# Wider mix pieces, sums over a whole row block, paired 64-row channel mixes, and output steps at later fixed places

## The chip, the cores and the metric

The kernel runs on one core of one Trainium2 chip. The metric is the device time of one execution in microseconds (us), as a median over the runs of a kernel. Engine names are those of the profile: PE is the matmul engine, PEld its weight loads, DVE the vector engine, ACT the scalar engine, POOL and SP the two engines that issue most DMAs.

## The reference

```python
# x: (8, 4224, 192) f32; weight: (8 heads, 7 taps); theta, ch: (192, 192); tok_r, tok_i: (4224, 4224)
w = softmax(weight, axis=-1)
x = causal 7-tap convolution of x along the sequence, one set of taps per head of 24 channels
theta = x @ w_theta
zr, zi = x * cos(theta), x * sin(theta)
y = einsum('ts,bsd->btd', w_tok_r, zr) + einsum('ts,bsd->btd', w_tok_i, zi)
u = x + y
out = u + maximum(u @ w_ch, 0)
```

The cost is in the two token mixes: for each of the 33 blocks of 128 output rows, matmuls over 4224 tokens (33 chunks of 128) against 1536 columns (8 batches times 192 channels), twice.

## The kernel before

The 33 chunks are done in three passes of 11, because `zr` and `zi` are kept for only 22 chunks at a time. Each pass goes over all 33 row blocks; partial sums go to memory between passes. The first row block of pass 1 builds its chunks as it goes; the chunks of pass 2 and pass 3 are built in the shade of the pass before. In the last pass the output work (add x, transpose, mix channels, relu, store) runs beside the token mix.

The parts that matter here, with cuts marked:

```python
PC = 2 * D                       # a piece is 384 columns (2 batches); NP = 4 pieces in a row block
PASSES = (11, 11, 11)

pe_last = [None]
def pe(ins):                     # all PE instructions keep the order in which they are written
    if pe_last[0] is not None:
        tc.add_manual_dep(ins.ins, pe_last[0].ins.name, NOSYNC, reason="order")
    pe_last[0] = ins
    return ins
# DVE has no such order: the scheduler of the framework chooses the order of its queue

def channel_weights(w, name):    # 192 rows of w as 4 slots of 128 rows; slots 1 and 2 padded with zeros
    R = D - P                    # 64
    t = constp.tile([P, 4, D], BF16, name=name)
    nc.vector.memset(t[:, 1:3, :], 0.0)
    # ... four DMAs: w[0:128], w[128:192] | w[0:64] in the lower half, w[64:192]
    return t

def channel_mix(dst, tT, w):     # 2 batches: 4 matmuls of 128 rows
    for b in range(2):
        for k in range(2):
            pe(nc.tensor.matmul(
                dst[:, b, :], lhsT=tT[:, b + k, :], rhs=w[:, 2 * b + k, :],
                start=(k == 0), stop=(k == 1),
            ))

def mix(y, wts, zs, c, j, ncs):  # one "mix step": chunk c of piece j, two matmuls
    # ...

def finish_piece(tb, j, y, p):
    # ... p == 0: copy y to ev, store; p == 1: load pv, ev = y + pv, store
    pv = wk.tile([P, PC], F32, name="pv", tag="pv", bufs=3)
    nc.sync.dma_start(out=pv, in_=part[p - 1][tb, :, cols])
    # ... last pass from here on:
    xr = wk.tile([P, PC], BF16, name="xr", tag="sn")
    nc.sync.dma_start(out=xr, in_=xs[rows, cols])
    nc.vector.tensor_tensor(out=pv, in0=pv, in1=xr, op=ALU.add)      # "the add"
    nc.vector.tensor_tensor(out=ev, in0=y, in1=pv, op=ALU.add)       # "the sum"
    ub = wk.tile([P, PC], BF16, name="ub", tag="cs")
    nc.scalar.activation(out=ub, in_=ev, func=AT.Copy)
    def transposes():            # 3 PE transposes of ub, DVE copies them to uT
        # ...
    def channels():              # channel_mix(v, uT, wch); ov = max(v, 0) + ev; store
        # ...
    return [transposes, channels]

# last pass: one output step half-way through a piece and one at its end
for c in range(ncs):
    mix(y, wts, zs[p], c, j, ncs)
    done += 1
    if pend and c in (ncs // 2, ncs - 1):
        pend.pop(0)()
    # ... cut
pend += finish_piece(tb, j, y, p)
```

Once per row block, DVE also transposes the mix weights of the next block (six instructions, `wt<-st`: four of 128x512 and two of 128x384).

## Time and profile before

| | us |
|---|---|
| median, the three runs given at first | 1712.29 |
| median, the same three and one more, set beside the changed kernel | 1710.88 (1706.91 to 1716.38) |
| profiled execution, span | 1714.9 |
| of it: first row block, with the first chunks' build | 119.2 |
| rest of pass 1 | 493.2 |
| pass 2 | 506.0 |
| last pass, to the start of the last PE instruction | 592.2 |
| tail, from that start to the end | 4.2 |

The stages are cut at the start of the mix matmul that begins each one. The page's first part gives the busy time of each engine with its share of the span and its instructions:

```profile
PE 1631.2 (95%) x11088; PEld 1004.9 (59%) x11088; DVE 886.7 (52%) x1737; ACT 237.2 (14%) x399; POOL 514.9 (30%) x948
```

The table of windows gives the same by stretch of time; its last three columns are the granted PE clock, the DMA share, and GB/s:

```profile
core 0: us, PE busy (x) PEld busy (x) DVE busy (x) ACT busy (x) POOL busy (x), PEclk, DMA share, GB/s
0.00:119.00 119.00, 76.68 (x572) 48.72 (x573) 75.50 (x146) 56.39 (x91) 55.52 (x104) 0.85 0.89 126
...
1118.00:1715.00 597.00, 555.67 (x3833) 342.94 (x3830) 344.29 (x720) 69.01 (x132) 130.72 (x244) 0.99 0.67 147
```

PE is full in the two middle stages (not shown) and idle for 42 us in the first and 41 us in the last. The list of waits names what PE and DVE waited for in the last pass (total us, times, longest):

```profile
PE tu L289 <- ACT ub L283: 24.8, 43, 2.2
PE v L225 <- DVE uT L290: 11.6, 32, 0.5
...
DVE pv L280 <- DMA pv<-part_84: 142.7, 96, 4.0
```

PE waits for the piece to be transposed and for the transposes to be copied. Behind both stands DVE, which waits for the load of `pv` in 96 of its 132 adds.

Busy time says little about PE, because matmuls overlap; the distance between starts says more. In the timeline (start, duration, engine, line, instruction, rows*columns of the weights, shape of what streams), a mix matmul of 384 columns starts 0.16 us after the one before. In the same trace are matmuls that use the array as two halves by columns (`96*64`), and each change of mode costs extra; a channel mix of two batches (`v`) has none:

```profile
420.70 0.33 PE L257 MATMUL y<-zi,wt_4149 128*128 128x384 bf16 x1
420.96 0.27 PE L170 MATMUL pc<-xw_3846,bands 96*64 96x192 bf16 x1
420.96 0.27 PE L170 MATMUL pc<-xw_3849,bands 96*64 96x192 bf16 x1
...
421.23 0.25 PE L170 MATMUL pc<-xw_3849,bands 96*64 96x192 bf16 x1
421.41 0.34 PE L257 MATMUL y<-zr,wt_4140 128*128 128x384 bf16 x1
...
1403.15 0.49 PE L225 MATMUL v<-wch,uT 128*128 128x192 bf16 x4
1403.48 0.33 PE L257 MATMUL y<-zr,wt_14563 128*128 128x384 bf16 x1
```

Over the whole trace the medians are: mix to mix 162.5 ns; a matmul of 192 columns to the next instruction 82.5 ns; a transpose 56 ns; mix to band matmul 256 ns where 162.5 would be normal; band to mix 178 ns where 82.5 would be. So each change of mode costs about 94 ns. The Trainium skill, "TensorE: Matmul & The Clock Gate", section Back-to-back issue gap, gives N/2.4 + 2.5 ns for N columns as the gap of isolated matmuls at the full clock; that is 162.5, 82.5 and 55.8 ns, which this trace agrees with.

These pitches add up to the time that the last pass would need without waits: 2904 mix matmuls of 162.5 ns, 396 transposes of 56 ns and 66 channel mixes at 660 ns (two mixes of two batches counted as one): 471.9 + 22.2 + 43.6 = 537.7 us. The pass takes 592.2 us, so about 54 us are waits.

### The profile page before, as it was taken

Reading aid. Unit: us, or ns where it says so; the run is one execution under the profiler, and the core shown is the slowest. Engines: PE = TensorE matmul, PEld = TensorE weight load, DVE = VectorE, ACT = ScalarE, POOL = GpSimd, SP = SyncE. Lnnn points to the kernel's source line nnn. Section 1 sums busy time; section 2 is a strip of 40 time slices with the busy share of each in tenths; the row PEclk is TensorE's granted clock in tenths of the full one; section 3 lists DMA queues with packets and bytes.
Section 4 is the critical chain, followed back from the end, with each engine's and each line's share of the span. In section 5 each row is a group of like instructions: output and inputs, shape, how many; then the busy total and the mean of one; then the engine's idle time right before and its main releaser. Section 6 shows DMA issues by size and latency. Waiting matters only on the chain. (4 is left out here: it accounts for less than half of the span.)

```text
span 1714.9 us, 28577 instructions
## 1 busy us (share of the span) xinstructions
PE 1631.2 (95%) x11088; PEld 1004.9 (59%) x11088; DVE 886.7 (52%) x1737; ACT 237.2 (14%) x399; POOL 514.9 (30%) x948
## 2 busy tenths in 40 slices
PE   4789999999999999999999999999999999999998
PEld 2446666666666666666666666655555555555555
DVE  6664444444444434444444444455565655656554
ACT  3541111111111001111111111001111111111111
POOL 6432333323333233333333223222122222221210
PEclk8889999999999999999999999999999999999999
DMA  9987766666666688878887877767677676676753
GB/s 120 138 135 139 125 118 124 120 123 117 116 114 121 119 161 175 164 173 172 181 177 165 172 161 161 163 149 153 151 150 154 149 152 152 144 158 149 155 134 97
DMA packets 305175, 248.75 MB, mean 145 GB/s; under 512 B 81168, under 2 KB 300816, under 8 KB 305040
## 3 DMA queue, kind: packets, MB, share of 16 engines
q0 software_dynamic: 167616, 91.14, 43.2%
q1 hardware_dynamic: 137424, 155.80, 28.8%
q8 instruction: 86, 1.41, 0.3%
q14 instruction: 49, 0.40, 0.1%
HBM read 247.07 MB, written 90.83 MB: 197 GB/s over the span
## 5 line engine op out<-in xcount | busy, mean ns | idle before, releaser
L238 POOL DMA_DIRECT2D st<-in_moe_w_tok_i_dram x396 | 212.8, 545 | 1006.2 <-DVE wt_15169 L247 14.5
L238 POOL DMA_DIRECT2D st<-in_moe_w_tok_r_dram x396 | 213.1, 546 | 10.8 <-issue 6.5
L215 ACT ACTIVATE cs<-ang,half_pi 128x768 bf16<-128x768 f32 x66 | 61.6, 933 | 653.6 <-DVE ang L208 653.5
L280 DVE TENSOR_TENSOR pv<-pv,xr 128x384 f32<-128x384 f32 x132 | 73.0, 553 | 147.3 <-DMA pv<-part_84 147.3
L283 ACT ACTIVATE ub<-ev 128x384 bf16<-128x384 f32 x132 | 69.0, 523 | 549.6 <-DVE ev L281 549.6
L275 DVE TENSOR_TENSOR ev<-y,pv 128x384 f32<-128x384 f32 x132 | 71.6, 542 | 137.4 <-PE y L257 133.0
L269 DVE COPY ev<-y 128x384 f32<-128x384 f32 x132 | 71.6, 542 | 135.5 <-PE y L257 135.3
L290 DVE COPY uT<-tu 128x384 bf16<-128x384 bf16 x132 | 46.0, 349 | 98.2 <-PE tu L289 98.2
L208 DVE TENSOR_SCALAR ang<-th 128x384 f32<-128x384 f32 x132 | 68.1, 549 | 51.7 <-PE th L225 49.9
L175 ACT ACTIVATE xz<-pc 128x384 bf16<-128x384 f32 x132 | 57.2, 485 | 262.7 <-PE pc L170 262.1
L225 PE MATMUL v<-wch,uT 128*128 128x192 bf16 x528 | 65.5, 247 | 11.6 <-DVE uT L290 11.6
L199 DVE COPY xT<-tp 128x768 bf16<-128x768 bf16 x66 | 36.4, 551 | 75.8 <-PE tp L195 75.5
L281 DVE TENSOR_TENSOR ev<-y,pv 128x384 f32<-128x384 f32 x132 | 72.2, 547 | 6.2 <-PE y L257 6.2
L296 DVE SCALAR_TENSOR_TENSOR ov<-v,ev 128x384 f32<-128x384 f32 x132 | 71.4, 541 | 0.6 <-PE v L225 0.6
L289 PE MATMUL tu<-ident,ub 128*128 128x128 bf16 x396 | 44.4, 221 | 25.7 <-ACT ub L283 24.8
L225 PEld LDWEIGHTS <-uT 128*128 128x128 bf16 x528 | 45.0, 98 | 36.7 <-DVE uT L290 23.7
L225 PE MATMUL th<-wth,xT 128*128 128x192 bf16 x528 | 61.5, 262 | 1.9 <-DVE ang L208 1.3
L289 PEld LDWEIGHTS <-ub 128*128 128x128 bf16 x396 | 28.0, 98 | 58.1 <-ACT ub L283 49.6
L225 PEld LDWEIGHTS <-xT 128*128 128x128 bf16 x528 | 50.4, 105 | 14.6 <-issue 7.0
L170 PEld LDWEIGHTS <-bands 96*64 96x64 bf16 x528 | 23.1, 112 | 54.6 <-issue 38.0
L216 ACT ACTIVATE sn<-ang 128x768 bf16<-128x768 f32 x66 | 54.6, 827 | 0.0
L217 DVE TENSOR_TENSOR zr<-xz,cs 128x768 bf16<-128x768 bf16 x66 | 36.6, 554 | 32.4 <-ACT cs L215 32.4
(761 smaller groups left out, 4336.7 us busy)
## 6 DMA issues: line engine op xcount, KB each, us to landing
st<-in_moe_w_tok_r_dram POOLq DMA_DIRECT2D x396, 88.0 KB, 5.0
st<-in_moe_w_tok_i_dram POOLq DMA_DIRECT2D x396, 88.0 KB, 3.5
part_83<-ev SPq DMA_DIRECT2D x132, 192.0 KB, 3.0
pv<-part_83 SPq DMA_DIRECT2D x132, 192.0 KB, 3.7
part_84<-ev SPq DMA_DIRECT2D x132, 192.0 KB, 3.3
pv<-part_84 SPq DMA_DIRECT2D x132, 192.0 KB, 2.6
out_dram<-ov SPq DMA_DIRECT2D x132, 192.0 KB, 2.6
xs<-xz SPq DMA_DIRECT2D x132, 96.0 KB, 4.1
```

The source lines that it names most:

```text
L175: nc.scalar.activation(out=xz[:, :, hp * 2 * G : (hp + 1) * 2 * G].rearrange("p b (h g) -> p h b g", h=2, g=G), in_=pc[:, :, :, :], func=A ...
L208: nc.vector.tensor_scalar(out=ang[:, k, :], in0=th[:, :, :].rearrange("p b d -> p (b d)"), scalar1=-CLAMP, scalar2=CLAMP, op0=ALU.max, op1 ...
L215: nc.scalar.activation(out=cs, in_=af, func=AT.Sin, bias=half_pi[:], scale=1.0)
L225: pe(nc.tensor.matmul(dst[:, b, :], lhsT=tT[:, b + k, :], rhs=w[:, 2 * b + k, :], start=(k == 0), stop=(k == 1),))
L238: nc.gpsimd.dma_start(out=st[a * Q : (a + 1) * Q, :, 0 : ncs * Q], in_=w[tb * P : (tb + 1) * P, t0 : t0 + ncs * Q].rearrange("(bt i) s -> ...
L269: nc.vector.tensor_copy(out=ev, in_=y)
L275: nc.vector.tensor_tensor(out=ev, in0=y, in1=pv, op=ALU.add)
L280: nc.vector.tensor_tensor(out=pv, in0=pv, in1=xr, op=ALU.add)
L281: nc.vector.tensor_tensor(out=ev, in0=y, in1=pv, op=ALU.add)
L283: nc.scalar.activation(out=ub, in_=ev, func=AT.Copy)
L289: pe(nc.tensor.transpose(tp[:, k, :], ub[:, k * P : (k + 1) * P], ident))
L296: nc.vector.scalar_tensor_tensor(out=ov, in0=v[:, :, :].rearrange("p b d -> p (b d)"), scalar=0.0, in1=ev, op0=ALU.max, op1=ALU.add,)
```

## The change

The intent has four parts. (1) A mix piece has 512 columns in place of 384: three pieces per row block and a quarter fewer matmuls. (2) `pv`, which holds the partial sums, is as wide as a row block, loaded ahead with one DMA, summed into in place and stored in two halves of four batches. The output steps of a row block stand at four fixed places, six to eight mix steps after their inputs. (3) A channel mix takes four batches. Where two batches' last 64 rows of contraction were padded to 128 with zeros, they are now two matmuls of 64 rows that can run side by side in the two halves of the array. (4) To fit, PSUM buffers go from 4+2+2 to 3+2x2+1 banks, so there is one buffer for transposes instead of two, and the clamp handles 768 columns at once.

The diff, cut to its core:

```diff
-    PC = 2 * D
+    PC = 512
 ...
-        t = constp.tile([P, 4, D], BF16, name=name)
-        nc.vector.memset(t[:, 1:3, :], 0.0)
+        t = constp.tile([P, 3, D], BF16, name=name)     # slot 1: 64 rows of each of the two cuts
 ...
-    trps = ctx.enter_context(tc.tile_pool(name="trps", bufs=2, space=bass.MemoryType.PSUM))
+    trps = ctx.enter_context(tc.tile_pool(name="trps", bufs=1, space=bass.MemoryType.PSUM))
 ...
     def channel_mix(dst, tT, w):
-        for b in range(2):
-            # 2 batches, 4 matmuls of 128 rows
+        R = D - P
+        for q in range(2):
+            v = [dst[:, k, q * D : (q + 1) * D] for k in range(2)]
+            for k in range(2):
+                pe(nc.tensor.matmul(
+                    v[k], lhsT=tT[:, 3 * q + 2 * k, :], rhs=w[:, 2 * k, :],
+                    start=True, stop=False,
+                ))
+            for k in range(2):
+                pe(nc.tensor.matmul(
+                    v[k], lhsT=tT[k * R : (k + 1) * R, 3 * q + 1, :],
+                    rhs=w[k * R : (k + 1) * R, 1, :], start=False, stop=True,
+                ))
 ...
+    def begin_rows(tb, p):
+        pv = wk.tile([P, N], F32, name="pv", tag="pv", bufs=3)
+        if p:
+            nc.sync.dma_start(out=pv, in_=part[p - 1][tb, :, :])
+        if p == len(PASSES) - 1:
+            # ... load xr
+            for j in range(NP):
+                nc.vector.tensor_tensor(                       # the add
+                    out=pv[:, cols], in0=pv[:, cols], in1=xr[:, cols], op=ALU.add
+                )
+        return pv
+
+    def finish_piece(tb, j, y, p, pv, ub):
+            nc.vector.tensor_tensor(out=pv[:, cols], in0=y, in1=pv[:, cols], op=ALU.add)   # the sum
+            # ... last pass: ACT copies to ub; other passes: store pv after the third piece
+
+    def output_steps(tb, pv, ub):
+        for g in range(NG):                                    # two groups of four batches
+            uT = transposed(ub[:, g * GC : (g + 1) * GC])
+            yield
+            channel_mix(v, uT, wch)
+            # ... pv = max(v, 0) + pv in two DVE operations, then store this half of pv
+            yield
 ...
+        places = (2 * ncs + 6, 3 * ncs + 1, 3 * ncs + 8, 4 * ncs + 3)   # mix steps from the block's start
 ...
+                if j == 0 and tb + 1 < NT:
+                    pv_next = begin_rows(tb + 1, p)            # written one row block ahead
```

More of the change, by code (lines that the diff above doesn't have):

```diff
@@ L40 @@
     NT = S // P
-    PC = 2 * D
+    PC = 512
     NP = N // PC
+    GB = 4
+    NG = B // GB
+    GC = GB * D
     PASSES = (11, 11, 11)
@@ L71 @@
     nc.sync.dma_start(out=wsb, in_=weight.partition_broadcast(P))
-    masks = wk.tile([2 * WR, KS, 2, Q], BF16, name="masks", tag="ev", bufs=3)
+    masks = wk.tile([2 * WR, KS, 2, Q], BF16, name="masks", tag="ang")
     nc.gpsimd.memset(masks, 1.0)
@@ L84, in channel_weights @@
         R = D - P
-        t = constp.tile([P, 4, D], BF16, name=name)
-        nc.vector.memset(t[:, 1:3, :], 0.0)
+        t = constp.tile([P, 3, D], BF16, name=name)
         nc.gpsimd.dma_start(out=t[:, 0, :], in_=w[0:P, :])
         nc.gpsimd.dma_start(out=t[0:R, 1, :], in_=w[P:D, :])
-        nc.gpsimd.dma_start(out=t[R:P, 2, :], in_=w[0:R, :])
-        nc.gpsimd.dma_start(out=t[:, 3, :], in_=w[R:D, :])
+        nc.gpsimd.dma_start(out=t[R:P, 1, :], in_=w[0:R, :])
+        nc.gpsimd.dma_start(out=t[:, 2, :], in_=w[R:D, :])
         return t
@@ L100 @@
     wpool = ctx.enter_context(tc.tile_pool(name="wpool", bufs=2))
-    yps = ctx.enter_context(tc.tile_pool(name="yps", bufs=4, space=bass.MemoryType.PSUM))
+    yps = ctx.enter_context(tc.tile_pool(name="yps", bufs=3, space=bass.MemoryType.PSUM))
     mmps = ctx.enter_context(tc.tile_pool(name="mmps", bufs=2, space=bass.MemoryType.PSUM))
-    trps = ctx.enter_context(tc.tile_pool(name="trps", bufs=2, space=bass.MemoryType.PSUM))
+    trps = ctx.enter_context(tc.tile_pool(name="trps", bufs=1, space=bass.MemoryType.PSUM))
     wmax = bpool.tile([P, H], F32, name="wmax")
@@ L122 @@
     )
-    btmp = wk.tile([2 * WR, H, 2 * Q], BF16, name="btmp", tag="pv", bufs=3)
+    btmp = wk.tile([2 * WR, H, 2 * Q], BF16, name="btmp", tag="xz")
     bview = bands[:, :, :, :].rearrange("p h a m -> p h (a m)")
@@ L164, in build_chunk @@
         xz = wk.tile([P, B, D], BF16, name="xz", tag="xz")
-        for hp in range(H // 2):
-            pc = mmps.tile([P, 2, B, G], F32, name="pc", tag="mm")
-            for hh in range(2):
-                h = 2 * hp + hh
+        for hp in range(H // 4):
+            pc = mmps.tile([P, 2, PC], F32, name="pc", tag="mm")
+            for hh in range(4):
+                h = 4 * hp + hh
                 for half in range(2):
                     pe(nc.tensor.matmul(
-                        pc[half * 2 * Q : (half + 1) * 2 * Q, hh, :, :],
+                        pc[half * 2 * Q : (half + 1) * 2 * Q, hh // 2,
+                           (hh % 2) * B * G : (hh % 2 + 1) * B * G],
                         lhsT=bands[:, h, :, :].rearrange("p a m -> p (a m)"),
@@ L174, in build_chunk @@
                     ))
-            nc.scalar.activation(
-                out=xz[:, :, hp * 2 * G : (hp + 1) * 2 * G].rearrange(
-                    "p b (h g) -> p h b g", h=2, g=G
-                ),
-                in_=pc[:, :, :, :], func=AT.Copy,
-            )
-            if hp % 2:
-                yield
+            for k in range(2):
+                h0 = (4 * hp + 2 * k) * G
+                nc.scalar.activation(
+                    out=xz[:, :, h0 : h0 + 2 * G].rearrange("p b (h g) -> p h b g", h=2),
+                    in_=pc[:, k, 0 : 2 * B * G].rearrange(
+                        "p (h b g) -> p h b g", h=2, b=B
+                    ),
+                    func=AT.Copy,
+                )
+            yield
         xf = xz[:, :, :].rearrange("p b d -> p (b d)")
@@ L189, in build_chunk @@
         zs.append((zr, zi))
-        HC = N // 2
         xTs = []
-        for j in range(2):
-            tp = trps.tile([P, 6, P], BF16, name="tp", tag="tr")
-            for k in range(6):
-                pe(nc.tensor.transpose(
-                    tp[:, k, :], xf[:, j * HC + k * P : j * HC + (k + 1) * P], ident
-                ))
-            xT = wk.tile([P, 6, P], BF16, name="xT", tag="xT")
-            nc.vector.tensor_copy(out=xT[:], in_=tp[:])
-            xTs.append(xT)
-            yield
@@ L202, in build_chunk @@
-        for j in range(2):
-            cols = slice(j * HC, (j + 1) * HC)
-            ang = wk.tile([P, 2, PC], F32, name="ang", tag="ang")
-            for k in range(2):
-                th = mmps.tile([P, 2, D], F32, name="th", tag="mm")
-                channel_mix(th, xTs[j][:, 3 * k : 3 * k + 3, :], wth)
-                nc.vector.tensor_scalar(
-                    out=ang[:, k, :], in0=th[:, :, :].rearrange("p b d -> p (b d)"),
-                    scalar1=-CLAMP, scalar2=CLAMP, op0=ALU.max, op1=ALU.min,
-                )
-            af = ang[:, :, :].rearrange("p k n -> p (k n)")
-            sn = wk.tile([P, HC], BF16, name="sn", tag="sn")
-            cs = wk.tile([P, HC], BF16, name="cs", tag="cs")
-            nc.scalar.activation(out=cs, in_=af, func=AT.Sin, bias=half_pi[:], scale=1.0)
-            nc.scalar.activation(out=sn, in_=af, func=AT.Sin)
-            nc.vector.tensor_tensor(out=zr[:, cols], in0=xf[:, cols], in1=cs, op=ALU.mult)
-            nc.vector.tensor_tensor(out=zi[:, cols], in0=xf[:, cols], in1=sn, op=ALU.mult)
-            yield
+        for g in range(NG):
+            xTs.append(transposed(xf[:, g * GC : (g + 1) * GC]))
+            yield
@@ new lines, in build_chunk @@
+        for g in range(NG):
+            cols = slice(g * GC, (g + 1) * GC)
+            th = mmps.tile([P, 2, PC], F32, name="th", tag="mm")
+            channel_mix(th, xTs[g], wth)
+            ang = wk.tile([P, GB, D], F32, name="ang", tag="ang")
+            nc.vector.tensor_scalar(
+                out=by_bank(ang[:, :, :]), in0=banks(th), scalar1=-CLAMP, scalar2=CLAMP,
+                op0=ALU.max, op1=ALU.min,
+            )
+            af = ang[:, :, :].rearrange("p b d -> p (b d)")
+            nc.scalar.activation(
+                out=zr[:, cols], in_=af, func=AT.Sin, bias=half_pi[:], scale=1.0
+            )
+            nc.scalar.activation(out=zi[:, cols], in_=af, func=AT.Sin)
+            for z in (zr, zi):
+                nc.vector.tensor_tensor(
+                    out=z[:, cols], in0=xf[:, cols], in1=z[:, cols], op=ALU.mult
+                )
+            yield
@@ L221, in channel_mix, with transposed @@
+    def transposed(u):
+        tp = trps.tile([P, 6, P], BF16, name="tp", tag="tr")
+        for k in range(6):
+            pe(nc.tensor.transpose(tp[:, k, :], u[:, k * P : (k + 1) * P], ident))
+        uT = wk.tile([P, 6, P], BF16, name="uT", tag="uT")
+        nc.vector.tensor_copy(out=uT[:], in_=tp[:])
+        return uT
     def channel_mix(dst, tT, w):
-        for b in range(2):
+        R = D - P
+        for q in range(2):
+            v = [dst[:, k, q * D : (q + 1) * D] for k in range(2)]
@@ L224, in channel_mix @@
             for k in range(2):
                 pe(nc.tensor.matmul(
-                    dst[:, b, :], lhsT=tT[:, b + k, :], rhs=w[:, 2 * b + k, :],
-                    start=(k == 0), stop=(k == 1),
-                ))
+                    v[k], lhsT=tT[:, 3 * q + 2 * k, :], rhs=w[:, 2 * k, :],
+                    start=True, stop=False,
+                ))
+            for k in range(2):
[3 more added lines that the diff above has]
+                ))
@@ L230, in mix_weights, with banks, by_bank @@
+    def banks(t):
+        return t[:, :, 0 : 2 * D].rearrange("p k (q d) -> p k q d", q=2)
+    def by_bank(t):
+        return t.rearrange("p (q k) d -> p k q d", k=2)
     def mix_weights(tb, p):
@@ L261, in mix @@
             ))
-    def finish_piece(tb, j, y, p):
-        cols = slice(j * PC, (j + 1) * PC)
-        rows = slice(tb * P, (tb + 1) * P)
-        ev = wk.tile([P, PC], F32, name="ev", tag="ev", bufs=3)
-        if p == 0:
-            nc.vector.tensor_copy(out=ev, in_=y)
-            nc.sync.dma_start(out=part[0][tb, :, cols], in_=ev)
-            return []
-        pv = wk.tile([P, PC], F32, name="pv", tag="pv", bufs=3)
-        nc.sync.dma_start(out=pv, in_=part[p - 1][tb, :, cols])
-        if p < len(PASSES) - 1:
-            nc.vector.tensor_tensor(out=ev, in0=y, in1=pv, op=ALU.add)
-            nc.sync.dma_start(out=part[p][tb, :, cols], in_=ev)
-            return []
-        xr = wk.tile([P, PC], BF16, name="xr", tag="sn")
-        nc.sync.dma_start(out=xr, in_=xs[rows, cols])
-        nc.vector.tensor_tensor(out=pv, in0=pv, in1=xr, op=ALU.add)
-        nc.vector.tensor_tensor(out=ev, in0=y, in1=pv, op=ALU.add)
-        ub = wk.tile([P, PC], BF16, name="ub", tag="cs")
-        nc.scalar.activation(out=ub, in_=ev, func=AT.Copy)
-        uT = wk.tile([P, 3, P], BF16, name="uT", tag="xT")
-        def transposes():
-            tp = trps.tile([P, 3, P], BF16, name="tu", tag="tr")
-            for k in range(3):
-                pe(nc.tensor.transpose(tp[:, k, :], ub[:, k * P : (k + 1) * P], ident))
-            nc.vector.tensor_copy(out=uT[:], in_=tp[:])
-        def channels():
-            v = mmps.tile([P, 2, D], F32, name="v", tag="mm")
-            channel_mix(v, uT, wch)
-            ov = wk.tile([P, PC], F32, name="ov", tag="ang")
-            nc.vector.scalar_tensor_tensor(
-                out=ov, in0=v[:, :, :].rearrange("p b d -> p (b d)"), scalar=0.0,
-                in1=ev, op0=ALU.max, op1=ALU.add,
-            )
-            nc.sync.dma_start(
-                out=out[2 * j : 2 * j + 2, rows, :].rearrange("b s d -> s b d"),
-                in_=ov[:, :].rearrange("p (b d) -> p b d", b=2),
-            )
-        return [transposes, channels]
@@ new lines, in begin_rows @@
+    def begin_rows(tb, p):
+        rows = slice(tb * P, (tb + 1) * P)
+        pv = wk.tile([P, N], F32, name="pv", tag="pv", bufs=3)
+        if p:
+            nc.sync.dma_start(out=pv, in_=part[p - 1][tb, :, :])
+        if p == len(PASSES) - 1:
+            xr = wk.tile([P, N], BF16, name="xr", tag="xz")
+            nc.sync.dma_start(out=xr, in_=xs[rows, :])
+            for j in range(NP):
+                cols = slice(j * PC, (j + 1) * PC)
+                nc.vector.tensor_tensor(
+                    out=pv[:, cols], in0=pv[:, cols], in1=xr[:, cols], op=ALU.add
+                )
+        return pv
@@ new lines, in finish_piece @@
+    def finish_piece(tb, j, y, p, pv, ub):
+        cols = slice(j * PC, (j + 1) * PC)
+        if p == 0:
+            nc.vector.tensor_copy(out=pv[:, cols], in_=y)
+        else:
+            nc.vector.tensor_tensor(out=pv[:, cols], in0=y, in1=pv[:, cols], op=ALU.add)
+        if p < len(PASSES) - 1:
+            if j == NP - 1:
+                nc.sync.dma_start(out=part[p][tb, :, :], in_=pv)
+        else:
+            nc.scalar.activation(out=ub[:, cols], in_=pv[:, cols], func=AT.Copy)
+    def output_steps(tb, pv, ub):
+        rows = slice(tb * P, (tb + 1) * P)
+        for g in range(NG):
+            uT = transposed(ub[:, g * GC : (g + 1) * GC])
+            yield
+            v = mmps.tile([P, 2, PC], F32, name="v", tag="mm")
+            channel_mix(v, uT, wch)
+            pg = pv[:, g * GC : (g + 1) * GC].rearrange("p (b d) -> p b d", d=D)
+            for k in range(2):
+                pk = by_bank(pg)[:, k, :, :]
+                nc.vector.scalar_tensor_tensor(
+                    out=pk, in0=banks(v)[:, k, :, :], scalar=0.0, in1=pk,
+                    op0=ALU.max, op1=ALU.add,
+                )
+            nc.sync.dma_start(
+                out=out[g * GB : (g + 1) * GB, rows, :].rearrange("b s d -> s b d"),
+                in_=pg,
+            )
+            yield
@@ L323, with chunk_major @@
     wch = channel_weights(moe_w_ch, "wch")
+    def chunk_major(tb, p, wts):
+        pv = begin_rows(tb, p)
+        ys = [yps.tile([P, PC], F32, name="y", tag="y") for _ in range(NP)]
+        for _ in range(5):
+            next(first, 0)
+        for c in range(PASSES[p]):
+            for j in range(NP):
+                next(first, 0)
+                next(first, 0)
+                mix(ys[j], wts, zs[p], c, j, PASSES[p])
+        for j in range(NP):
+            finish_piece(tb, j, ys[j], p, pv, None)
     for p, ncs in enumerate(PASSES):
@@ L331 @@
         done = 0
-        pend = []
+        pv_next = None
+        outs = []
         for tb in range(NT):
@@ L339 @@
             if p == 0 and tb == 0:
-                ys = [yps.tile([P, PC], F32, name="y", tag="y") for _ in range(NP)]
-                for _ in range(5):
-                    next(first, 0)
-                for c in range(ncs):
-                    for j in range(NP):
-                        next(first, 0)
-                        if j % 2:
-                            next(first, 0)
-                        mix(ys[j], wts, zs[0], c, j, ncs)
+                chunk_major(tb, p, wts)
                 done += NP * ncs
-                for j in range(NP):
-                    finish_piece(tb, j, ys[j], p)
                 continue
+            pv = pv_next or begin_rows(tb, p)
+            pv_next = None
+            ub = None
+            if last_pass:
+                ub = wk.tile([P, N], BF16, name="ub", tag="ang")
+                outs.append((done, list(places), output_steps(tb, pv, ub)))
             for j in range(NP):
@@ L356 @@
                     mix(y, wts, zs[p], c, j, ncs)
+                    for at, where, gen in outs:
+                        if where and done - at == where[0]:
+                            where.pop(0)
+                            next(gen)
                     done += 1
-                    if pend and c in (ncs // 2, ncs - 1):
-                        pend.pop(0)()
                     if taken < steps and done * steps * 20 >= total * 19 * taken:
@@ L362 @@
                         taken += 1
-                pend += finish_piece(tb, j, y, p)
-        for f in pend:
-            f()
+                finish_piece(tb, j, y, p, pv, ub)
+                if j == 0 and tb + 1 < NT:
+                    pv_next = begin_rows(tb + 1, p)
+            outs = [o for o in outs if o[1]]
+        for at, where, gen in outs:
+            for _ in where:
+                next(gen)
         for _ in side:
```

## The prediction

> **What bounds the kernel now.** The page gives PE 1631 us of a 1715 us span (95%), DVE 52%. The table of windows shows PE full from 150 to 1130 us; idle PE lies in the first 120 us (a latency chain, about 9.3 us per chunk) and in the last pass. In the timeline, matmuls of 384 columns start 162.5 ns apart, of 192 columns 82.5: 2.4 columns per ns plus about 2.5 ns each. So 8712 mix matmuls are 1416 us and each channel mix 44 us. Gaps above those pitches sum to about 56 us in the first 150 us and 52 us in the last pass: 34 us from a mix to the output transposes (the list of waits: PE tu on ACT ub), 16 us from a mix to the output channel mix (PE v on DVE uT). There ub is late because DVE waits in order for pv.
>
> **What changes, costed.**
>
> 1. Mix matmuls of 512 columns: 6534 instead of 8712. Estimate 512/2.4+2.5 = 215.8 ns each, 1410 us: −6 us.
>
> 2. Output steps at fixed places, 6 to 8 mix steps (0.43 us each) after their inputs, and pv loaded a row block ahead: nearly all of the 52 us of waits go. I count −50 us. DVE's backlog (finish 0.7, six weight transposes 3.9, two output operations 1.1, one copy 0.55 us) just fits in front of the second channel mix, at about 6.9 us.
>
> 3. Channel mixes: for four batches, 4 matmuls of 128 rows and 2 pairs of 64 rows in place of 8 of 128 rows. If a pair overlaps (the band matmuls already run as pairs 4 ns apart, one pair per 82.5 ns), streaming falls from 660 to about 503 ns: −21 us over 132 mixes. But each mix goes into and out of the 64-row tiling twice. The Trainium skill, "TensorEngine Tiling (Array Packing)", section Key Properties, says that changing the tiling mode drains the engine. This trace agrees for the band matmuls' column tiling: mix to band 255 ns in place of 163, band to mix 178 in place of 82.5, so about 94 ns each way. Four switches of 94 ns on 132 mixes: +50 us. Net +29 us. Row tiling's own switch is in no record here; this is the main uncertainty.
>
> 4. Start: one transpose buffer and one 768-column clamp lengthen the chain per chunk by 0.3 to 0.6 us: +4 us. End: more output work follows the last mix: +2 us.
>
> All of this lies on PE, the critical path, so it adds up: 1712 − 6 − 50 + 29 + 6 = about 1690; I lean a little lower, for cheaper switches: **1687 us, range 1642 to 1700**. Chances: faster by over 2% 0.33, within 2% 0.64, slower 0.03.
>
> **What would show each step.** (1) Mix matmuls starting 216 ns apart. (2) No PE waits on ub and uT in the list, PE full in the last pass. (3) In a channel mix, about 175 ns from the last 128-row matmul to the first 64-row one and back again, the pair 4 ns apart, about 880 ns from its first matmul to the next mix. (4) A first row block some us longer.
>
> **What would make it wrong.** Row-tiling switches without a drain: about 1640. Pairs that don't overlap: +22 us. pv or the weight transposes holding DVE so long that the fixed places come too early: part of the 50 us stays.

## The result and the profile after

The changed kernel took **1778.86 us** (median of four runs, 1777.71 to 1782.79), against 1710.88 for the kernel before. The ratio is 1.0399, with a 95% interval of 1.0365 to 1.0433. Here and below, a ratio is the mean time of one kernel's fast runs over that of the other's of the same rounds, so it is not quite the ratio of the medians. It is 4% slower where 1.5% faster was predicted, and far outside the range. The results were correct in this and every other run.

By stage, from the profiled executions (us):

| | before | after | difference |
|---|---|---|---|
| first row block | 119.2 | 130.5 | +11.3 |
| rest of pass 1 | 493.2 | 497.5 | +4.3 |
| pass 2 | 506.0 | 510.0 | +4.0 |
| last pass | 592.2 | 637.6 | **+45.4** |
| tail | 4.2 | 5.2 | +1.0 |

The page and the same windows as before:

```profile
PE 1667.8 (94%) x8910; PEld 767.8 (43%) x8910; DVE 857.3 (48%) x1471; ACT 229.3 (13%) x366; POOL 517.5 (29%) x948
```

```profile
core 0: us, PE busy (x) PEld busy (x) DVE busy (x) ACT busy (x) POOL busy (x), PEclk, DMA share, GB/s
0.00:130.00 130.00, 93.61 (x549) 42.90 (x550) 71.34 (x121) 55.20 (x91) 55.83 (x104) 0.64 0.83 115
...
1138.00:1781.00 643.00, 566.41 (x3103) 261.60 (x3101) 325.76 (x587) 62.37 (x99) 131.67 (x244) 0.99 0.58 133
```

PE is now idle for 77 us of the last pass, in place of 41. The list of waits of the last pass shows the same three kinds as before, all longer in total, and the queue of the SP engine, which issues the loads of `pv` (L289):

```profile
PE tp L223 <- ACT ub L310: 42.9, 29, 5.8
PE v L235 <- DVE uT L225: 28.4, 28, 1.0
...
DVE pv L295 <- DMA pv<-part_84: 168.8, 32, 8.6
...
SPq L289 <- DMA out_dram<-pv: 166.3, 30, 7.8
```

There are about 30 of each in 33 row blocks: it is one wait per row block. DVE waits for a load, and the load waits for an output DMA that must first empty its buffer.

The two matmul costs can be read off the timeline. This is one channel mix of four batches and the two mix matmuls after it:

```profile
1515.98 0.34 PE L235 MATMUL v<-wch,uT 128*128 128x192 bf16 x2 [1.04 <-DVE uT L225]
1516.25 0.26 PE L240 MATMUL v<-wch,uT 64*128 64x192 bf16 x2
1516.44 0.34 PE L235 MATMUL v<-wch,uT 128*128 128x192 bf16 x2
1516.71 0.26 PE L240 MATMUL v<-wch,uT 64*128 64x192 bf16 x2
1516.90 0.39 PE L278 MATMUL y<-zr,wt_11551 128*128 128x512 bf16 x1
1517.12 0.38 PE L278 MATMUL y<-zi,wt_11560 128*128 128x512 bf16 x1
```

Mix matmuls are 215.8 ns apart over the whole trace, as predicted. The channel mix takes 910 ns by the median over the trace, where two mixes of two batches took 660. One that starts after a wait of PE, like this one (1515.98 to 1516.90), takes about 10 ns more, as it does in the kernel before and in e2; the expectations use its 919 ns. Inside, by medians over the trace: 83 ns from the first 128-row matmul to the second (93 after a return from a pair, or after a wait), 178 ns from the second to the first 64-row one, 3 to 4 ns within a pair, and 185 ns from the pair back to 128 rows.

With these the last pass without waits is 2178 x 215.8 ns + 396 x 56 ns + 66 x 910 ns = 470.0 + 22.2 + 60.1 = 552.3 us. It took 637.6, so about 85 us are waits, 31 us *more* than before. The +45.4 us of the pass is −1.9 (pieces) + 16.5 (channel mixes) + 31 (waits).

The chain of waits around one row block shows where the waits come from (start, us, engine and what). Small pieces are left out:

```profile
1499.48 6.12 DMA out_dram<-pv
...
1505.73 4.09 DMA pv<-part_84
...
1509.94 0.10 DVE pv L295
...
1510.55 0.03 DVE pv L305
...
1511.15 1.75 DVE wt_11694 L268 x3
1512.90 1.65 DVE wt_11703 L268 x3
1514.55 0.91 DVE pv L323 x2
1515.46 0.47 DVE uT L225
...
1517.72 0.94 DVE pv L323 x2
...
1518.68 6.35 DMA out_dram<-pv
```

It begins and ends with the same kind of event, the output DMA of a row block, 19.2 us later. In between: output DMA 6.3 us with its hand-over, load of `pv` 4.2 us, and 8.7 us on DVE. PE's own work for a row block is 552.3 / 33 = 16.7 us, so this loop and not PE sets the pace of the last pass: 33 x 19.2 = 634 us. The two transfers in it are larger than before, and slower to land: by the pages' medians, 4.2 us for the 768 KB of a `pv` load (2.6 us for 192 KB before) and 5.0 us for 384 KB of output (2.6 us for 192 KB).

The timeline of DVE shows why a *load* can hold up the *current* block:

```profile
1509.94 0.69 DVE L295 TENSOR_TENSOR pv<-pv,xr 128x512 f32<-128x512 f32 x1 [5.09 <-DMA pv<-part_84]
1510.55 0.68 DVE L305 TENSOR_TENSOR pv<-y,pv 128x512 f32<-128x512 f32 x1
```

L295 is the add of a block that is not needed yet. L305 is the sum of the third piece of block t, whose matmuls are done, and on which the transposes, the output mix and the output DMA of block t depend. L295 stands in front of it and waits 5 us for its load. In the built program's order, L295 belongs to block t+2: the source writes it one block ahead, and the scheduler moved it ahead by one more. The trace confirms it: counted in the order in which DVE ran them in the last pass, this L295 is the first add of block 20 (from 0), and this L305 the third sum of block 18. Block t+2 takes the buffer of block t−1 (three buffers), so its load waits until block t−1's output has left. The loop is closed: output of t−1 → load of t+2 → add of t+2 → (queue order) third sum of t → output of t. The Trainium skill, "Perfetto Trace Analysis", section Tensor Engine Instruction (MATMUL, LD_WEIGHTS), says that DVE and ACT are strict first-in-first-out; the trace agrees: the last mix matmul of that third piece ended at 1505.98, so in about 4.0 of the 5.09 us DVE stood idle while L305 could have run.

### The profile page after: what moved, and what is told of

It is laid out like the page before. It is cut to its first block, busy times and chain, and to the rows that moved or that the text cites. A ratio compares the mean times of both kernels' runs of the same rounds, so it can differ in the third digit from the quotient of the medians.

```text
span 1780.6 us, 22353 instructions
## 1 busy us (share of the span) xinstructions
PE 1667.8 (94%) x8910; PEld 767.8 (43%) x8910; DVE 857.3 (48%) x1471; ACT 229.3 (13%) x366; POOL 517.5 (29%) x948
## 4 chain that ended last, share of the span: by engine, by line
PE 59%; DMA 18%; DVE 13%; issue 2%; DVEq 0%; ACT 0%; SPq 0%
PE y L278 54%; DMA out_dram<-pv 10%; DMA pv<-part_84 8%; DVE pv L323 3%; DVE pv L295 2%; PE pc L172 1%; PE th L235 1%; DVE pv L305 1%; PE tp L223 1%; PE th L240 1%; DVE uT L225 1%; DMA part_84<-pv 1%; PE v L235 0%; PE v L240 0%; DVEq L268 0%
## 5 line engine op out<-in xcount | busy, mean ns | idle before, releaser
L305 DVE TENSOR_TENSOR pv<-y,pv 128x512 f32<-128x512 f32 x198 | 134.8, 681 | 156.9 <-PE y L278 156.8
L225 DVE COPY uT<-tp 128x768 bf16<-128x768 bf16 x132 | 72.7, 551 | 169.8 <-PE tp L223 169.5
L295 DVE TENSOR_TENSOR pv<-pv,xr 128x512 f32<-128x512 f32 x99 | 67.0, 680 | 177.2 <-DMA pv<-part_84 177.2
L209 ACT ACTIVATE zr<-ang,half_pi 128x768 bf16<-128x768 f32 x66 | 61.6, 933 | 671.0 <-DVE ang L204 671.0
L310 ACT ACTIVATE ub<-pv 128x512 bf16<-128x512 f32 x99 | 62.4, 630 | 600.8 <-DVE pv L305 600.8
L303 DVE COPY pv<-y 128x512 f32<-128x512 f32 x99 | 67.2, 678 | 109.8 <-PE y L278 109.7
L204 DVE TENSOR_SCALAR ang<-th 128x768 f32<-128x768 f32 x66 | 62.8, 952 | 96.4 <-PE th L240 96.1
L223 PE MATMUL tp<-ident,ub 128*128 128x128 bf16 x396 | 38.0, 220 | 42.9 <-ACT ub L310 42.9
L235 PE MATMUL v<-wch,uT 128*128 128x192 bf16 x264 | 44.4, 250 | 28.4 <-DVE uT L225 28.4
L323 DVE SCALAR_TENSOR_TENSOR pv<-v,pv 128x384 f32<-128x384 f32 x132 | 66.0, 539 | 7.3 <-PE v L240 7.3
L212 ACT ACTIVATE zi<-ang 128x768 bf16<-128x768 f32 x66 | 54.6, 828 | 0.0
L235 PE MATMUL th<-wth,uT 128*128 128x192 bf16 x264 | 51.0, 281 | 0.0
```

Source lines behind the costliest of these rows:

```text
L204: nc.vector.tensor_scalar(out=by_bank(ang[:, :, :]), in0=banks(th), scalar1=-CLAMP, scalar2=CLAMP, op0=ALU.max, op1=ALU.min,)
L209: nc.scalar.activation(out=zr[:, cols], in_=af, func=AT.Sin, bias=half_pi[:], scale=1.0)
L223: pe(nc.tensor.transpose(tp[:, k, :], u[:, k * P : (k + 1) * P], ident))
L225: nc.vector.tensor_copy(out=uT[:], in_=tp[:])
L235: pe(nc.tensor.matmul(v[k], lhsT=tT[:, 3 * q + 2 * k, :], rhs=w[:, 2 * k, :], start=True, stop=False,))
L295: nc.vector.tensor_tensor(out=pv[:, cols], in0=pv[:, cols], in1=xr[:, cols], op=ALU.add)
```

## The experiments

Twelve kernels were run. Each experiment's ratio is to the kernel before, timed in the same rounds; diffs are against the changed kernel unless said otherwise. Where the expectations call a theory by a letter, A (in its final form A2) is that DVE's wait for `pv` holds PE up, through the order of DVE's queue as above. The rivals are that the fixed places come too early for the work in front of them (B), that the larger transfers saturate the DMA queues (C), and that the paired mixes do the harm. About 2.6% of the mix matmul records are missing from the traces of e5 to e8 and e10; their times are not touched by that.

| run | what | us | ratio (95%) |
|---|---|---|---|
| changed kernel | | 1778.86 | 1.0399 (1.0365–1.0433) |
| e1_pv4 | a fourth `pv` buffer | 1777.53 | 1.0381 (1.0353–1.0408) |
| e2_padded | padded channel mixes | 1765.59 | 1.0313 (1.0282–1.0344) |
| e3_later | places 12 steps later | 1702.72 | 0.9953 (0.9931–0.9975) |
| e4_pv4_padded | e1 + e2 | 1761.12 | 1.0289 (1.0268–1.0311) |
| e5_ordered | DVE order alone | 1700.18 | 0.9930 (0.9912–0.9948) |
| e6_later_two_switches | e3 + half as many mode changes | 1678.60 | 0.9805 (0.9787–0.9824) |
| e7_later_padded | e3 + e2 | 1671.46 | 0.9762 (0.9743–0.9780) |
| e8_later_padded_start | e7 + other steps in the start | 1672.07 | 0.9775 (0.9753–0.9798) |
| e9_before_later | kernel before, later steps | 1715.25 | 1.0015 (0.9996–1.0035) |
| e10_ordered_padded | e5 + e2 | **1667.79** | 0.9738 (0.9718–0.9759) |
| e11_before_ordered | kernel before, DVE order | 1683.97 | 0.9848 (0.9833–0.9863) |
| e12_before_ordered_later | e9 + e11 | 1685.43 | 0.9855 (0.9839–0.9872) |

### e1_pv4: a fourth buffer

```diff
-        pv = wk.tile([P, N], F32, name="pv", tag="pv", bufs=3)
+        pv = wk.tile([P, N], F32, name="pv", tag="pv", bufs=4)
```

> The changed kernel with four pv buffers in place of three, nothing else; the order of instructions on DVE stays the same. Theory A (a closed loop in the last pass: the output DMA of a row block frees the pv buffer, then the pv load, then the pv+xr add that stands in DVE's queue in front of the third piece's sum, then DVE's backlog up to the output; 6.3+4.2+8.7 = 19.2 us per row block, above the 16.9 us of PE work): the load no longer waits for the output just issued, the last pass falls from 638 to about 557 us, the waits of PE on ub go, total about 1700 us, ratio to before about 0.993. Theory B (the fixed places come too early for DVE's own backlog of about 8.7 us, whatever the DMA does): the waits stay, ratio about 1.03 to 1.04. Theory C (DMA queues saturated by the large transfers): no change, 1.04.

The time did not move (1.0381 against 1.0399; last pass 635.6 against 637.6 us). The order of DVE's queue was expected to stay, and that was a miss: with a fourth buffer the scheduler moved the load and the add one more block ahead, so that the add of t+3, not of t+2, stands in front of the third sum of t (in its trace, the first add of block 21 runs just before the third sum of block 18). Block t+3 with four buffers again takes the buffer of t−1. The chain of waits of this run shows the same loop with the same parts, 19.6 us from output DMA to output DMA:

```profile
1518.27 6.43 DMA out_dram<-pv
...
1524.83 4.12 DMA pv<-part
...
1529.17 0.45 DVE pv L295
...
1537.90 5.79 DMA out_dram<-pv
```

So a wait for a buffer is not always cured by another buffer.

### e2_padded: the channel mixes padded to 128 rows

```diff
-        t = constp.tile([P, 3, D], BF16, name=name)
+        t = constp.tile([P, 4, D], BF16, name=name)
+        nc.vector.memset(t[:, 1:3, :], 0.0)
 ...
-            for k in range(2):   # two of 128 rows, then a pair of 64 rows
+            for b in range(2):
+                for k in range(2):
+                    pe(nc.tensor.matmul(
+                        v[b], lhsT=tT[:, 3 * q + b + k, :], rhs=w[:, 2 * b + k, :],
+                        start=(k == 0), stop=(k == 1),
+                    ))
```

> The changed kernel with the zero-padded 128-row channel mixes of before, nothing else. A channel mix goes from about 919 ns back to about 660 ns (eight matmuls 82.5 ns apart), so the passes 1 and 2 lose about 4 us each and the first row block some us. Theory A (last pass bound by the DMA and DVE loop of 19.2 us, not by PE): the last pass keeps its 638 us, PE waits grow instead; ratio about 1.032. Rival (mixes and waits simply add up): the last pass loses 17 us as well, ratio about 1.02.

The padded mixes bring 1.0399 down to 1.0313. By stage, against the changed kernel: start −3.6, pass 1 −5.4, pass 2 −5.8, last pass −4.4 us. In the two middle passes, PE is full and there are 22 channel mixes in each: 22 x 0.250 us = 5.5 us, as seen. In the last pass there are 66, worth 16.5 us, but only 4.4 us show. The rest turned into waiting:

```profile
PE tp L224 <- ACT ub L307: 53.5, 29, 6.9
```

In the changed kernel that wait was 42.9 us. A faster PE only waits longer for a loop that it is not part of.

### e3_later: places twelve steps later

```diff
-        places = (2 * ncs + 6, 3 * ncs + 1, 3 * ncs + 8, 4 * ncs + 3)
+        places = (2 * ncs + 6 + 12, 3 * ncs + 1 + 12, 3 * ncs + 8 + 12, 4 * ncs + 3 + 12)
```

> The changed kernel with every output step 12 mix steps (about 5 us) later, three pv buffers. The built order shows that the scheduler then puts the pv+xr adds behind the first piece's sum of a row block rather than in front of the third's. Theory A: the loop is broken up or shortened to about 16 us, under PE's 16.9, so the last pass falls to 560 to 590 us, total 1700 to 1730. Theory B: later places cure it fully, about 1700. Theory C (DMA saturated): 1.04 as the changed kernel.

The time drops by 76 us to 0.9953. The last pass goes from 637.6 to 558.1 us, almost to the 552.3 us that PE needs, and PE's two waits shrink to 1.1 and 1.4 us. That alone would also fit "the places were too early". But the edit changed two things: in the built order the scheduler now puts the adds behind the sum of the first piece (in the trace, the adds of block 23 run behind the first sum of block 22). This run cannot tell the two apart; e5 can.

### e4_pv4_padded: both e1 and e2

The edit is that of e1 and of e2 together.

> Both of the first two. Theory A: with the loop gone PE bounds the last pass and the padded mixes now pay there as well: last pass about 540 us, total about 1672 us, ratio about 0.976, against about 0.993 for four buffers alone. Theories B and C: about 1.02 to 1.03.

It came out at 1.0289 where 0.976 was expected: a clear miss, for the reason seen in e1. The last pass is still 628.4 us.

### e5_ordered: the order of DVE's queue, and nothing else

```diff
+    sum_last = [None]
 ...
-                nc.vector.tensor_tensor(
+                add = nc.vector.tensor_tensor(
                     out=pv[:, cols], in0=pv[:, cols], in1=xr[:, cols], op=ALU.add
                 )
+                if sum_last[0] is not None:
+                    tc.add_manual_dep(
+                        add.ins, sum_last[0].ins.name, NOSYNC, reason="order"
+                    )
 ...
-            nc.vector.tensor_tensor(out=pv[:, cols], in0=y, in1=pv[:, cols], op=ALU.add)
+            sum_last[0] = nc.vector.tensor_tensor(
+                out=pv[:, cols], in0=y, in1=pv[:, cols], op=ALU.add
+            )
```

> The changed kernel with its own places and three pv buffers; only an order edge on DVE: the pv+xr adds of the next row block stand behind the latest sum of a piece (in the built order: behind the first piece's sum, no longer in front of the third's). Four buffers did not help, because the scheduler used the fourth to put the load and the add one row block further ahead, at the same spot of the loop. Theory A2 (the add that waits for its load, placed in DVE's in-order queue in front of the third piece's sum, closes the 19.2 us loop): last pass from 638 to about 557 us, total about 1702 us, ratio about 0.995. Theory B (the places are too early for DVE's backlog): waits of PE on ub and uT stay, ratio 1.02 to 1.04.

The places, the three buffers and every operation are those of the changed kernel. Only an ordering edge, without any semaphore, keeps each add behind the sum that is written before it. The time drops to 0.9930. In the list of waits of PE for 1150 to 1690 us, both waits are gone and one line is left:

```profile
PE y L278 <- issue: 1.9, 12, 0.2
```

The timeline of DVE shows a sum, which waited for nothing but its matmuls, and then three adds that wait for nothing:

```profile
1511.28 0.69 DVE L311 TENSOR_TENSOR pv<-y,pv 128x512 f32<-128x512 f32 x1 [0.30 <-PE y L278]
1511.88 1.89 DVE L297 TENSOR_TENSOR pv<-pv,xr 128x512 f32<-128x512 f32 x3
```

This settles it: at the same places and with the same buffers, the waits vanish when the queue's order is mended. The places were not too early. Nor were the DMA queues saturated (C): the same transfers now fit into a shorter pass, with a DMA share of 0.66 (window 1131 to 1693 us) where the changed kernel's last pass had 0.58.

### e6_later_two_switches and e7_later_padded: what the 64-row pairs cost

e6 is e3 with the second half of each channel mix mirrored, so that its 64-row pair follows that of the first half; the array changes mode twice per mix, not four times. e7 is e3 with the padded mixes of e2.

```diff
-            for k in range(2):   # 128 rows
-            for k in range(2):   # 64 rows
+            for part64 in (q == 1, q == 0):
+                for k in range(2):
+                    rows = slice(k * R, (k + 1) * R) if part64 else slice(0, P)
+                    i = 1 if part64 else 2 * k
+                    pe(nc.tensor.matmul(
+                        v[k], lhsT=tT[rows, 3 * q + i, :], rhs=w[rows, i, :],
+                        start=part64 == (q == 1), stop=part64 == (q == 0),
+                    ))
```

> The later places (1703 us) and in each channel mix the second half mirrored, so that the two 64-row pairs stand together: two changes of tiling per mix in place of four, the same matmuls. If each change costs about 100 ns, a mix goes from 919 to about 711 ns, the middle passes lose 4.6 us each, the last pass 14, total about 1677 us, ratio about 0.980. If the cost belongs to the 64-row matmuls themselves and not to the change of tiling: no gain, 0.995.

> The later places and the zero-padded 128-row mixes of before. Here PE bounds the last pass, so the padded mixes should now pay in it (they gave 4 us there while the loop bound it): mixes 660 ns, last pass about 541 us in place of 558, middle passes 5.7 us less each, total about 1671 us, ratio about 0.977. If the loop still held: about 1690.

Measured 0.9805 (expected 0.980) and 0.9762 (expected 0.977). From the timelines of e6 and then of e7, a channel mix of four batches takes about 0.71 us with two changes of mode (1449.94 to 1450.65; median 708 ns) and 0.66 us padded (1438.79 to 1439.45; median 660 ns):

```profile
1449.94 0.87 PE L238 MATMUL v<-wch,uT 128*128 128x192 bf16 x8
1450.65 0.38 PE L276 MATMUL y<-zr,wt 128*128 128x512 bf16 x1
```

```profile
1438.79 0.82 PE L237 MATMUL v<-wch,uT 128*128 128x192 bf16 x8
1439.45 0.38 PE L275 MATMUL y<-zr,wt 128*128 128x512 bf16 x1
```

(An answer that joins instructions prints the first one's form for all; the eight of e6 are four of 128 rows and four of 64.) With 910, 708 and 660 ns for four, two and no changes, two changes cost about 202 ns. If four cost twice that, a paired mix without any would take 506 ns, so the streaming that two pairs save is about 154 ns (an estimate), and it does not pay for even one round trip.

### e8_later_padded_start: the start

e8 is e7 with the build's steps spread differently between the mixes of the first row block:

```diff
-                next(first, 0)
-                next(first, 0)
+                for _ in range((3, 1, 2)[j]):
+                    next(first, 0)
```

> As the run before, and in the first row block a mix piece stands between the two groups of six transposes, which share one PSUM buffer. Theory for the first row block's extra 11 us: with one buffer the second group waits for the DVE copy of the first (7 us in the list of waits), and nothing stands between. Expected: first row block from about 127 to about 120 us, total about 1664, ratio about 0.973. Rival: the start is bound by the chain through ACT and DVE; then no change, 0.977.

It was expected at 0.973 and came out at 0.9775, no better than e7: a miss. From the end of the first chunk to that of the eleventh, the build takes 10.1 us per chunk on average, against 9.9 in e7 and 9.3 in the kernel before. The wait that it aimed at, PE's transposes on the copy `uT`, did shrink (7.2 us in e7's start, 0.9 here), but PE's wait for `xz` from ACT grew by more (15.7 to 28.4 us). The spread of the PE's steps is not what limits the chunk.

### e9_before_later: only later output steps, in the kernel before

```diff
-                    if pend and c in (ncs // 2, ncs - 1):
+                    if len(pend) > 2 and c in (ncs // 2, ncs - 1):
```

(against the kernel before)

> The kernel before with one edit: an output step is taken one piece (11 mix steps, about 3.6 us) later than it was. Nothing of the rest of the change. If the 52 us of PE waits on ub and uT in its last pass come from steps placed too soon after their inputs, they go: last pass from 592 to about 542 us, total about 1662 us, ratio about 0.971, which would beat every kernel so far. If an add that waits for its load holds DVE there as well, part of the waits stays: 0.98 to 1.0.

Five rounds give 1.0015: no change, where 0.971 was expected; the alternative, that an add holds DVE there as well, was put at 0.98 to 1.0. PE's wait for `ub` (24.8 us) is gone, but its wait for `uT` grew from 11.6 us to this:

```profile
PE v L225 <- DVE uT L290: 40.4, 34, 2.6
```

DVE still waits 154 us for loads of `pv`. The wait moved to the next step. Later steps in the kernel before do not help while DVE is held.

### e10_ordered_padded: the better version

The edits of e5 and e2 together.

> The changed kernel with the order edge on DVE and the zero-padded mixes, at its own places. The two cures should add up, because PE bounds the last pass now: 1700 minus 17 in the last pass, minus 11 in the middle passes, minus 3 in the first row block: about 1669 us, ratio about 0.975, as with the later places and padded mixes (0.976).

1667.79 us, 0.9738 in five rounds. It beats both the kernel before and the changed kernel and is the fastest measured. Only two PE waits of 0.7 us are left between 1150 and 1690 us. It is not told apart from e7 (0.9762), whose interval overlaps.

### e11_before_ordered and e12_before_ordered_later: the same cause in the kernel before

```diff
-        nc.vector.tensor_tensor(out=pv, in0=pv, in1=xr, op=ALU.add)
-        nc.vector.tensor_tensor(out=ev, in0=y, in1=pv, op=ALU.add)
+        add = nc.vector.tensor_tensor(out=pv, in0=pv, in1=xr, op=ALU.add)
+        if sum_last[0] is not None:
+            tc.add_manual_dep(add.ins, sum_last[0].ins.name, NOSYNC, reason="order")
+        sum_last[0] = nc.vector.tensor_tensor(out=ev, in0=y, in1=pv, op=ALU.add)
```

(against the kernel before; e12 has the edit of e9 as well)

> The kernel before with only the order edge on DVE: the pv+xr add of a piece stands behind the previous piece's sum, where before it stood in front of it. If the 52 us of waits in its own last pass come from the same thing as in the changed kernel (an add that waits for its load holds DVE in front of the sum that PE's output steps need), the waits of PE on ub mostly go; what is left is the 3.4 us of weight transposes once per row block: about 1670 to 1685 us, ratio about 0.98. If the steps are simply too soon after their inputs: 1.00.

> The kernel before with the order edge and with each output step one piece later (which alone gave nothing, 1.0015). With DVE no longer held by loads, the later steps should now hide the weight transposes too: last pass from 592 to about 542 to 550 us, total 1662 to 1670 us, ratio 0.971 to 0.976, as good as the changed kernel with order edge and padded mixes (0.974). If the waits stay, the order edge is not the cause in the kernel before.

The order edge alone makes the kernel before 1.5% faster, at the slow end of what was expected (1670 to 1685 us); its last pass takes 558.3 us in place of 592.2. From the lists of waits of PE and DVE in the last pass of e11:

```profile
PE v L225 <- DVE uT L294: 11.6, 32, 0.5
PE tu L293 <- ACT ub L287: 1.0, 1, 1.0
...
DVE pv L282 <- DMA pv<-part: 5.2, 1, 5.2
```

The 24.8 us for `ub` are 1.0, and DVE's 142.7 us for `pv` are 5.2. So the greater part of the waits that the prediction wanted to remove by moving steps came from the order of DVE's queue already. e12 was expected at 0.971 to 0.976 and gave 0.9855, the same as e11: a miss. Its one wait, PE on `uT`, is 15.3 us in 33 times, once per row block. In e12's timeline the copy to `uT` stands behind five of the weight transposes (2.79 us), and moving both output steps together leaves the distance between them as it was. That last reason is read from the trace and was not tested.

## Why the prediction was wrong

**The step that failed** is step 2: "Output steps at fixed places, 6 to 8 mix steps (0.43 us each) after their inputs, and pv loaded a row block ahead: nearly all of the 52 us of waits go. I count −50 us." The waits did not go; they grew from about 54 to about 85 us, where −50 was counted. That is 81 of the 92 us between 1687 and 1779.

What the runs showed in its place: loading `pv` further ahead did not free DVE from the load. The scheduler used the freedom to put the add of a block still further ahead in front of the sum that the current block needs. As the load for that add waits for the output of an earlier block's buffer, a loop of 19.2 us per row block closed, longer than PE's 16.7 us. e5 changes the order alone and removes it (1.0399 to 0.9930); e1 shows that one more buffer does not (1.0381). Two parts of the step held: the diagnosis of the kernel before ("There ub is late because DVE waits in order for pv"), which e11 confirms, and the places themselves, which are late enough once the order is mended (e5).

The material was there before the change ran. The built order has the add in front of the third sum, but the prediction does not mention it. Following that load back to the buffer it takes, and from there to the output DMA that frees it, would have shown the loop. With durations from the trace before (DVE's six weight transposes 3.8 us and the rest) its length could have been estimated. The prediction's last paragraph did name the risk ("pv or the weight transposes holding DVE so long that the fixed places come too early"), but as a part of the 50 us that stays, not as something that grows.

**Step 1 was right.** Mix matmuls start 215.8 ns apart, and 6534 of them are 5.7 us cheaper than 8712 before.

**Step 3 had the right mechanism, and was a little low in size.** The estimate was about 880 ns per channel mix of four batches (+29 us over 132); it is 910 ns, +0.250 us each or +33 us. The way into the 64-row mode costs about 96 ns, the way back about 103, and the second 128-row matmul after a return comes 93 instead of 82.5 ns later. The pairs do overlap, 3 to 4 ns apart. The Trainium skill, "TensorEngine Tiling (Array Packing)", section Key Properties, says that changing the tiling mode drains the engine. This trace agrees in so far as each change costs time: 178 and 185 ns where 82.5 would be normal. Padding (e7 against e3) and half as many changes (e6) confirm it from the other side.

**Step 4 was right in direction, and low.** The start is 11.3 us longer, not 4; the tail 1.0, not 2. About 3.6 us of the start are the paired mixes (e2). The other 7 or so stay open: one transpose buffer and the 768-column clamp lengthen the chain per chunk in my reading, but no run isolates them, and e8 did not shorten it. The granted clock, 0.64 in this stretch against 0.85 before, is not the cause: in e5 the last chunk of the start was ready at nearly the same time (129.6 us against 129.2) with a clock of 1.00 throughout.

The sum, in us: −5.7 (pieces) + 27.5 (110 channel mixes outside the start, 0.250 each) + 31 (waits) + 11.3 (start) + 1 (tail) = about 65. The two profiled executions differ by 66, the medians by 68.

## What to carry to other kernels

Where an engine runs its queue in order, ask of each operation that has been moved ahead what it waits for, all the way back: through its load to the buffer, and through the buffer to the store that frees it. If that store hangs on something later in the same queue, there is a loop, and its length, not the busiest engine, is the time per turn; more buffers may only let the scheduler move the operation further ahead, while an order edge that costs nothing removes it. And price a switch of mode per visit, not per matmul: here two pairs saved about 154 ns of streaming and one way in and out cost about 202, so padding was cheaper. By these numbers it would take three pairs per visit to pay (an estimate; no run has three).

## What the Trainium skill lacked or had wrong

- "TensorEngine Tiling (Array Packing)", section Key Properties, says that a change of mode drains the engine but gives no price. Here it is about 94 ns each way for column halves, and about 96 ns in and 103 ns back for row halves. Its section Theoretical Speedup gives up to 2x for a contraction of 64 or less; with two pairs of 192 columns in a mix of four batches, the mix went from 660 ns padded to 910 ns with four changes and 708 ns with two.
- "TensorE: Matmul & The Clock Gate", section Back-to-back issue gap, gives sustained spacings of about 131 ns at N=512 and about 81 ns at N=128 for streams in which every matmul has its weight load, and calls N/2.4 + 2.5 ns the gap of isolated matmuls. Here every matmul has a weight load (11088 of each before, 8910 of each after), and the streams keep to the second formula: 215.8 ns at 512, 162.5 at 384, 82.5 at 192 and 56 at 128 columns (transposes, in short runs).
- "Perfetto Trace Analysis", section Optimization Strategy, says of gaps that repeat that they can mean too little room for the next tile (buffer count, tile sizes). Here a gap that repeats once per row block was not cured by a fourth buffer (1.0381 against 1.0399) but by the order of an in-order queue (0.9930). None of the pages I read describes such a loop of store, buffer, load and queue order (19.2 us per turn, against 16.7 us of PE work).
